# DeltaNet in chunks of 64 with hash-routed experts: a new order for the first phase, unread products in idle time, Gram blocks laid out by ScalarE, a narrower join and another opening

## The chip, the cores and the metric

The kernel runs on one core of a Trainium2 chip. The metric is the device time of one execution in microseconds (us), from runs of the same kernel. TensorE (PE) multiplies, VectorE (DVE) and ScalarE (ACT) work element by element, GpSimd (POOL) fills, copies and issues its own DMAs, SyncE (SP) issues most DMAs. Each engine carries out its instructions in the order in which they were emitted, and waits at one whose inputs are not there.

## The reference

Attention first: 4 batches and 8 heads make 32 independent recurrences over 768 tokens with a 48x48 state each. Then every token goes through the one expert that a hash of its id picks.

```python
k_n = k / (norm(k) + 1e-6)
for t in range(768):
    y[t] = q[t] @ state
    state = state + beta[t] * outer(k_n[t], v[t] - k_n[t] @ state)
x = y.transpose(0, 2, 1, 3).reshape(3072, 384)       # 8 heads x 48 side by side
e = (token_id * 2654435761) % 8
out = relu(x @ w1[e]) @ w2[e]                        # w1: 8x384x1024, w2: 8x1024x384
```

## The kernel before

**Two phases.** The first computes the attention and scatters the rows of `x`, sorted by expert, to `x_scratch` in DRAM. The second takes the experts one after the other: two dense matrix products each (lines L993 and L1023), with the result scattered to the output (L1030). It begins when the last row of `x` has been written and read back.

**The first phase by chunks.** The 768 tokens are cut into 12 chunks of 64 (`NU`), and two chunks make a group (`GC`), so there are 6 groups. On the partitions stand 64 tokens of each of two batches; the other two batches (`g2`) and the heads stand in the free dimension. For every chunk:

- `load` brings K, Q and V by DMA (L343), `turn` transposes K and Q on PE (L359) and ACT copies them to SBUF (`KQ`, L366).
- `gram` makes K K^T and K Q^T (PE, L386). The 64x64 Gram matrix of a chunk is kept as four 32x32 blocks. ACT copies the upper right block to `N12` (L398) and the left column, times a mask, to `GK` (L402); then DVE adds the lower right block into `GK` (L406), so that `GK` holds the two diagonal blocks. DVE masks K Q^T to `MT` (L411).
- `inverse`, once a group: DVE transposes `GK` to `NT` (L438), makes norms and factors (L440 to L465, with one root on ACT, L444), and inverts the 32x32 triangular blocks in 31 steps of two instructions each (L475 product into `tmp`, L473 sum into `U`). Each step needs the one before. `U` was filled with zeros by ACT (L435). `turn_back` transposes `U` on DVE to `TN` (L488) and `TU` (L490).
- `join` puts two 32x32 inverses together to one of 64x64, `TT`: PE L505, ACT to `Z` (L524), PE L514, ACT to the right half of `TT` (L530). The left half is a masked ACT copy of `TU` (L519). `Z` has an identity in its right half, so that the second product writes the upper right block and the lower right block in one go (64 rows).
- `chunk` is the recurrence: `ask` reads the state with K (PE L543), DVE subtracts from V (`R`, L558; V was scaled in L424), PE multiplies by `TT` (L566), ACT copies `W` (L577), PE updates the state (L588), ACT copies it to `S` in four pieces (L602). The answers `psY` (L543 with Q, L566 with `MT`) go by ACT to `x_sb` (L612), POOL adds the row's number (L617) and scatters it (L618).

Buffers tie the groups together: there are two `U`, one `TU` and one `TN`, four `N12`, five `KQ` and five `MT`. So group g+2 can't be inverted before group g has been turned back and joined.

**The order.** No engine's order is written by hand. Every piece of work is a `task` with an engine, a cost in ns, what it reads and writes; `order()` plays the tasks through with these costs and gives the sequence in which they are emitted. A task's priority is the length of the chain of work behind it (`rest`). There is no clock in it: a product costs the same at all times. A task of `routing` (L645, one DVE chain that sorts the tokens) takes part like the others. Matrix products that need a PSUM bank take one of those that are free at that moment.

**The opening.** POOL makes the identity and fills `S` and `x_sb` with zeros (L805, L807). ACT issues eight small DMAs for the token ids (L895), then one for `beta` (L900). DVE converts index tables (L910, L911).

Of the kernel before, what the change touches and what calls it, by code (L numbers as in the profile page):

```python
# [13 lines left out]
ACT = mybir.ActivationFunctionType  # L14
ALU = mybir.AluOpType
# [5 lines left out]
def kernel(  # L21
# [79 lines left out]
    with ExitStack() as phase1:  # L101
# [10 lines left out]
        SEED, SPREAD, PATIENCE = 1, 0.0, 0.2  # L112
        N_K, N_Q, N_V, N_KQ, N_MT, N_N = 5, 2, 3, 5, 5, 4
# [31 lines left out]
        Zs = tiles(1, "Z", [P, NS, CK])  # L145
# [41 lines left out]
        def task(eng, ns, reads, writes, emit, words=0, kb=0, more=0, boost=0, job=None,  # L187
                 hold=0, claim=(), room=()):
            deps = {writer[r] for r in reads if r in writer}
            for w in (*writes, *room):  # L190
                deps |= readers.get(w, set())
                if w in writer:
# [5 lines left out]
                              claim=claim))  # L198
# [18 lines left out]
        def order():  # L217
# [17 lines left out]
            rest = [x + t["boost"] + chance.uniform(-SPREAD, SPREAD)  # L235
# [12 lines left out]
            done = []  # L248
# [20 lines left out]

            while len(done) < n:  # L270
                best, can = None, {}
# [9 lines left out]
                pick = max((i for x, i in r if x <= at), key=lambda i: rest[i])  # L281

                soon = [x for x, i in r
                        if at < x < at + PATIENCE * tasks[pick]["ns"] and rest[i] > rest[pick]]
                if soon:
                    fits = [i for x, i in r if x <= at and tasks[i]["ns"] <= min(soon) - at + 60]
                    if fits:
                        pick = max(fits, key=lambda i: rest[i])
                    else:
                        free[e] = min(soon)  # L290
                        continue
                t = tasks[pick]
                ready[e] = [p for p in ready[e] if p[1] != pick]
                s = at
                if t["words"]:
# [7 lines left out]
                    issued += t["words"]  # L303
                start[pick] = s
                for b in t["claim"]:
                    banks[b] = None
                free[e] = s + t["ns"]
                end[pick] = s + t["ns"]
# [24 lines left out]
            return sorted(done, key=lambda i: (start[i], i)), start  # L333
# [16 lines left out]
        def turn(what, c, g2):  # L350
# [6 lines left out]
            def go():  # L357
                for u in range(HU):
# [4 lines left out]
            task("PE", 560, held(what, n, c, (g2,)), (f"j{job}",), go, words=8, job=job,  # L363
                 room=(f"KQ{c % N_KQ}.{a}.{g2}",))
            task("ACT", 490, (f"j{job}",), (f"KQ{c % N_KQ}.{a}.{g2}",),
                 lambda: nc.scalar.activation(KQ[:, HU * g2:HU * g2 + HU, a], view(), ACT.Copy),  # L366
                 job=job)

        def gram(c, g2, parts=(0, 1)):
# [4 lines left out]
            job = new_job(2 if parts == (0,) else 1 if parts == (1,) else 3,  # L374
                          early=c < 6, pair=True)
# [6 lines left out]
            def go():  # L382
                for u in range(HU):
# [7 lines left out]
            task("PE", 1000 if len(parts) == 2 else 600, need, (f"j{job}",), go, words=64, job=job,  # L391
                 room=((f"N{c % N_N}.{g2}", f"GK{g % 2}.{cc}.{g2}") if 0 in parts else ())
                 + ((f"MT{c % N_MT}.{g2}",) if 1 in parts else ()))
            gk = GK[:, :, x0:x0 + H]
            n12 = N12[:, H * g2:H * g2 + H]
            if 0 in parts:
                task("ACT", 320, (f"j{job}",), (f"N{c % N_N}.{g2}",),
# [733 lines left out]
```

## Time and profile before

| | us |
|---|---|
| runs | 600.21, 607.21, 607.65 (median 607.21) |
| profiled execution | 604.45 |
| its span, first to last instruction | 602.9 |
| PE, DVE, ACT, POOL busy | 496.7, 276.2, 140.2, 136.9 |

The span is cut below into stretches that begin and end where a group of inverses is done. Busy times of DVE are unions: neighbours overlap by about 0.1 us, so the distance between two starts is shorter than the duration. [...]

### The profile page before, as it was taken

The page shows a single profiled execution, that of the slowest core. Times are in us where ns is not written, and L with a number is a line of the kernel's source. Part 1 is how long each engine was busy: PE and PEld are TensorE (multiplying, and loading weights), DVE is VectorE, ACT ScalarE, POOL GpSimd, SP SyncE. Part 2 cuts the span into 40 slices and gives each one's busy share as a digit, 9 for nine tenths or more (in the row PEclk, how much of TensorE's full clock was granted, in tenths as well). Part 3 has the DMA queues.
Part 4 walks back from the last instruction along what each step waited for, and adds up shares of the span by engine and source line. Part 5 has one row for each costly group of instructions (what it writes and reads, how often), then busy time and mean ns, then how long its engine had stood idle before and what let it go on. Part 6 is the DMA issues. An engine that isn't in the chain of part 4 may idle for free. (4 is left out here: it accounts for less than half of the span.)

```text
span 602.9 us, 14839 instructions
## 1 busy us (share of the span) xinstructions
PE 496.7 (82%) x6340; PEld 385.1 (64%) x6340; DVE 276.2 (46%) x740; ACT 140.2 (23%) x271; POOL 136.9 (23%) x160
## 2 busy tenths in 40 slices
PE   4960399988299798549895799999999999999992
PEld 3850398877289788448794466565757676767650
DVE  6689976888984486994200122211212121212100
ACT  4451145554134563213331000101000000000000
POOL 3002301110000110100112001707161525252531
PEclk9995558898756986855888699999999999999996
DMA  5674022453113231010612985426170808000001
GB/s 105 124 138 113 2 42 67 91 115 65 45 29 77 63 82 42 28 22 22 205 64 73 289 235 145 151 51 232 33 256 12 274 13 276 12 24 14 26 23 27
DMA packets 106019, 55.85 MB, mean 93 GB/s; under 512 B 93364, under 2 KB 102013, under 8 KB 105056
## 3 DMA queue, kind: packets, MB, share of 16 engines
q1 hardware_dynamic: 100240, 45.12, 30.1%
q0 software_dynamic: 5472, 9.65, 4.5%
q8 instruction: 50, 0.82, 0.6%
q10 hardware_dynamic: 240, 0.12, 0.1%
q14 instruction: 17, 0.14, 0.1%
HBM read 44.51 MB, written 10.62 MB: 91 GB/s over the span
## 5 line engine op out<-in xcount | busy, mean ns | idle before, releaser
L993 PE MATMUL h_ps<-xT,w_sb 128*128 128x424 f32 (+3 forms) x384 | 130.3, 500 | 11.0 <-DMA xr<-x_scratch 11.0
L1030 POOL DMA_INDIRECT out_dram<-o_sb,idx x90 | 87.6, 973 | 162.7 <-DVE o_sb L1025 90.2
L993 PEld LDWEIGHTS h_ps<-xT,w_sb 128*128 128x128 f32 x384 | 74.3, 194 | 65.0 <-issue 27.8
L1023 PE MATMUL o_ps<-h_sb,w_sb 128*128 128x424 f32 (+3 forms) x336 | 112.3, 494 | 0.0
L1023 PEld LDWEIGHTS o_ps<-h_sb,w_sb 128*128 128x128 f32 x336 | 84.4, 251 | 27.2 <-issue 0.3
L618 POOL DMA_INDIRECT x_scratch<-x_sb,slot x24 | 24.1, 1006 | 232.0 <-ACT x_sb L612 188.5
L996 ACT ACTIVATE h_sb<-h_ps 128x424 f32<-128x424 f32 (+3 forms) x32 | 15.9, 497 | 233.5 <-PE h_ps L993 233.5
L998 DVE TENSOR_SCALAR h_sb<-h_ps 128x424 f32<-128x424 f32 (+3 forms) x32 | 18.1, 564 | 109.3 <-PE h_ps L993 109.3
L475 DVE TENSOR_TENSOR tmp<-U,Ni 128x112 f32<-128x112 f32 (+15 forms) x186 | 60.6, 336 | 2.5
L473 DVE TENSOR_TENSOR U<-U,tmp 128x112 f32<-128x112 f32 (+15 forms) x186 | 60.6, 337 | 2.4
L1025 DVE STREAM_TRANSPOSE o_sb<-o_ps 128x384 f32<-128x384 f32 (+2 forms) x21 | 15.5, 738 | 84.3 <-PE o_ps L1023 84.3
L505 PE MATMUL psZ<-TN,N 32*32 32x32 f32 x448 | 12.0, 218 | 33.5 <-DVE TN L488 32.8
L558 DVE TENSOR_TENSOR R<-V,psX 128x384 f32<-128x384 f32 x22 | 12.0, 547 | 51.7 <-PE psX L543 32.7
L505 PEld LDWEIGHTS psZ<-TN,N 32*32 32x32 f32 x448 | 10.7, 132 | 34.9 <-DVE TN L488 21.7
L566 PE MATMUL psX<-R,TT 64*64 64x48 f32 x704 | 29.9, 248 | 3.5 <-DVE R L558 1.9
L566 PE MATMUL psY<-W,MT 64*64 64x48 f32 x768 | 31.9, 240 | 0.0
L566 PEld LDWEIGHTS psX<-R,TT 64*64 64x64 f32 x704 | 28.0, 164 | 5.5 <-ACT root L444 2.1
L566 PEld LDWEIGHTS psY<-W,MT 64*64 64x64 f32 x768 | 29.2, 156 | 2.2 <-issue 1.2
L386 PE MATMUL psZ<-KQ 48*64 48x128 f32 (+1 forms) x576 | 24.9, 321 | 6.0 <-ACT N L398 4.0
L543 PE MATMUL psX<-S,KQ 128*64 128x96 f32 x352 | 25.9, 305 | 2.4 <-ACT S L602 2.4
L617 POOL COPY x_sb<-number 128x4 f32<-128x4 f32 x24 | 14.2, 590 | 49.4 <-DVE U L473 49.3
L386 PEld LDWEIGHTS psZ<-KQ 48*64 48x64 f32 x576 | 19.8, 166 | 8.3 <-ACT N L398 5.2
(155 smaller groups left out, 582.1 us busy)
## 6 DMA issues: line engine op xcount, KB each, us to landing
w_sb<-in_moe_w_dram SPq DMA_DIRECT2D x14, 1536.0 KB, 12.1
K<-in_k_dram SPq DMA_DIRECT2D x48, 96.0 KB, 3.1
Q<-in_q_dram SPq DMA_DIRECT2D x48, 96.0 KB, 3.2
V<-in_v_dram SPq DMA_DIRECT2D x48, 96.0 KB, 2.7
xr<-x_scratch SPq DMA_DIRECT2D x16, 145.5 KB, 3.3
w_sb<-in_moe_w_dram SPq DMA_DIRECT2D x3, 512.0 KB
w_sb<-in_moe_w_dram SPq DMA_DIRECT2D x4, 384.0 KB, 9.4
out_dram<-o_sb,idx POOLq DMA_INDIRECT x90, 2.2
```

Source lines behind the costliest of these rows:

```text
L386: nc.tensor.matmul(view()[rows(p), r, u, a0:a1], lhsT=KQ[half(r), HU * g2 + u, 0, rows(p)], rhs=KQ[half(r), HU * g2 + u, a0:a1, rows(p)], ...
L473: nc.vector.tensor_tensor(U[:, n:, 0:n], U[:, n:, 0:n], t, op=ALU.add)
L475: nc.vector.tensor_tensor(t, U[:, j:n, 0:n].to_broadcast([P, m, n]), Ni[:, j, n:, None].to_broadcast([P, m, n]), op=ALU.mult)
L505: nc.tensor.matmul(bank(one)[part(p, 1), C * x:C * x + C], lhsT=N12[part(p, 0), x], rhs=TN[part(p, 0), x0 + x], start=(x == 0), stop=True, ...
L543: nc.tensor.matmul(out[rows(p), 2 * D * u:2 * D * u + 2 * D], lhsT=KQ[:, HU * g2 + u, a, rows(p)], rhs=S0[:, p, HU * g2 + u], start=(u == ...
L566: nc.tensor.matmul(out[rows(p), D * h:D * h + D], lhsT=left[rows(p), H * g2 + h], rhs=right[rows(p), g2, D * h:D * h + D], start=(fresh an ...
L618: put = nc.gpsimd.indirect_dma_start(out=x_dram[:, :], out_offset=bass.IndirectOffsetOnAxis(ap=slot[:, col:col + 1], axis=0), in_=x_sb.rea ...
L993: nc.tensor.matmul(h_ps[:, :width], lhsT=w1_sb[:, co, fo * P:(fo + 1) * P], rhs=xT[:, co, :width], start=(co == 0), stop=(co == CO - 1))
L996: nc.scalar.activation(h_sb[:, fo, :width], h_ps[:, :width], ACT.Relu)
L998: nc.vector.tensor_scalar(out=h_sb[:, fo, :width], in0=h_ps[:, :width], scalar1=0.0, scalar2=None, op0=ALU.max)
L1023: nc.tensor.matmul(os_ps[i][:, 0:width], lhsT=w2_sb[:, fo, i::CO], rhs=h_sb[:, fo, 0:width], start=(fo == 0), stop=(fo == FO - 1))
L1030: scat = nc.gpsimd.indirect_dma_start(out=out_q, out_offset=bass.IndirectOffsetOnAxis(ap=idx[e][:, k:k + 1], axis=0), in_=o_sb[:, k], in_o ...
```

## The change

- **Costs and clock in the planner.** Task costs are set anew (for example products of 64 rows 980 ns for 1050). `order()` keeps a sum of the recent work of PE (`act` of each task), and takes 1.85 times the cost where this sum is below `warm` (after 30 us of plan time). Changing the kind of product costs 150 ns; staying with a kind gets a bonus in priority.
- **Priorities.** Each task has a tag and each tag an addition to its priority (`boosts`, from -204000 to 596500 ns). On DVE the head of an inverse and its steps stand highest, `MT` loses its place above all others, V is low. On ACT `S` and `W` stand above `GK` and `x`.
- **DVE's patience.** DVE waits for a more urgent task up to 45 ns; before, up to a fifth of the task at hand.
- **Unread products.** Where the plan leaves PE idle for over 260 ns (or has it slow) and the sum is short, after 40 us of plan time, a 128x128x128 product of the identity with itself is put into a free bank. Nobody reads it.
- **Gram blocks by ACT.** The masked ACT copy and the DVE addition (L402, L406) become three ACT copies: the left column for all partitions, then the lower right block over it for partitions 32 to 63 and 96 to 127.
- **Narrower join.** `Z` loses its identity half, the second product writes 32 rows. The lower right block comes into `TT` by a second masked ACT copy of `TU`; the upper right one by two ACT copies of 32 partitions.
- **Opening.** `beta` comes first on ACT's queue; the eight DMAs of the token ids go to POOL's queue, behind the index tables. POOL fills `U`; ACT fills `S` and `x_sb`, from 24 us of plan time on. The identity in `Z` is not made.

```diff
+        boosts = {"GK": 378500, "KQ": -25500, "MT": 67000, "N12": -30000, "R": 51500,
+                  "S": 596500, "TT": -146500, "TT12": 292000, "V": -28000, "W": 443000,
+                  "Z": -204000, ..., "head": 496000, "late": 2500, "own": 28500,
+                  "route": 134000, "solve": 500, "step": 344500, ..., "x": 374500}
...
-            rest = [x + t["boost"] + chance.uniform(-SPREAD, SPREAD)
+            rest = [x + t["boost"] + boosts.get(t["tag"], 0) + chance.uniform(-SPREAD, SPREAD)
...
+            def rate(x):
+                return 1.0 if activity(x) >= model["warm"] or x < 30000 else 1.85
...
+                span = model["wait"] if e == "DVE" else PATIENCE * tasks[pick]["ns"]
...
+                if e == "PE":
+                    gap = at - free[e]
+                    short = model["warm"] * 1.15 - activity(at)
+                    b = choices(dict(pair=False, early=False))
+                    if (at > model["fill"] and b and b[0] <= free[e] and short > 0
+                            and (gap > 260 or rate(at) > 1) and (gap > 260 or t["act"] < 0.45 * t["ns"])):
+                        ns = 215 * rate(free[e])
+                        ...
+                            tasks.append(dict(eng="PE", ns=ns, tag="fill", kind="full", at_bank=at_bank,
+                                              emit=lambda at_bank=at_bank: unread(at_bank)))
...
+        def unread(at_bank):
+            nc.tensor.matmul(homes[at_bank][:, 0:P], lhsT=ident, rhs=ident, start=True,
+                             stop=True, skip_group_check=True)
...
+                for i, (at, col) in enumerate(((slice(0, P), 0), (part(0, 1), C),
+                                               (part(1, 1), C))):
+                    task("ACT", 400, ..., lambda at=at, col=col: nc.scalar.activation(
+                             gk[at], view()[at, :, :, 0, col:col + C], ACT.Copy),
+                         job=job, tag="GK")
-                task("ACT", 400, ..., lambda: nc.scalar.activation(
-                         gk.rearrange("p j (u r) -> p r u j", r=2), view()[:, :, :, 0, 0:C],
-                         ACT.Copy, scale=kmask[:, 0:1]), job=job)
-                task("DVE", 340, ..., lambda: nc.vector.scalar_tensor_tensor(
-                         out=gk.rearrange("p j x -> p x j"), in0=n12, scalar=kmask[:, 1:2],
-                         in1=gk.rearrange("p j x -> p x j"), op0=ALU.mult, op1=ALU.add))
-                task("DVE", 600, ..., boost=1e6, job=job)            # MT
+                task("DVE", 610, ..., job=job, tag="MT")
...
-            task("ACT", 900, (), (f"U{i}",), lambda: nc.scalar.activation(
-                U, zero[:, :, None].to_broadcast([P, C, C]), ACT.Copy))
+            task("POOL", 1000, (), (f"U{i}",), lambda: nc.gpsimd.memset(U, 0.0))
...
-                            bank(two)[rows(p), C * x:C * x + C], lhsT=Z[part(p, 1), x],
+                            bank(two)[part(p, 0), C * x:C * x + C], lhsT=Z[part(p, 1), x],
...
+            for s_ in range(2):
+                task("ACT", 610, ("TU",), (f"TT{c % 3}.{s_}",), lambda s_=s_: nc.scalar.activation(
+                    TT[:, :, C * s_:C * s_ + C], TU[:, x0:x0 + NS], ACT.Copy,
+                    scale=kmask[:, s_:s_ + 1]), tag="TT")
+            for p in range(2):
+                task("ACT", 500, (f"j{two}", f"TT{c % 3}.1"), (f"TT{c % 3}.{2 + p}",),
+                     lambda p=p: nc.scalar.activation(TT[part(p, 0), :, C:], ...), tag="TT12")
...
-            dv("tensor_copy", rows_i, frm, more=9000, **on)
+            dv("tensor_copy", rows_i, frm, more=3000, **on)
...
+            nc.scalar.dma_start(out=beta_h, in_=beta.rearrange("b h s -> (b h) s"))
             make_identity(nc, ident)
...
-                        nc.scalar.dma_start(
+                        nc.gpsimd.dma_start(
                             out=tid32[w:w + NTC].rearrange("(c g) i w -> g c i w", g=2)[g2],
```

## Rows read from the trace of the kernel before

**Rows 1.** The page's span in 40 equal slices of 15.1 us: busy tenths of DVE and the granted clock of PE in tenths.
```profile
DVE  6689976888984486994200122211212121212100
...
PEclk9995558898756986855888699999999999999996
```

**Rows 2.** Busy time of each engine by stretch (us from the span's start), cut where inverses are done; then granted clock, DMA share and GB/s. In brackets the number of instructions.
```profile
30.00:75.00 45.00, 16.12 (x293) 13.28 (x295) 41.95 (x141) 12.08 (x24) 8.95 (x1) 0.66 0.42 85
75.00:110.00 35.00, 33.06 (x774) 30.20 (x768) 24.63 (x74) 17.12 (x33) 2.55 (x4) 0.66 0.29 59
110.00:163.00 53.00, 39.26 (x958) 34.61 (x954) 47.32 (x149) 22.13 (x45) 7.48 (x12) 0.88 0.38 82
163.00:208.00 45.00, 39.84 (x986) 37.39 (x988) 25.90 (x51) 20.26 (x38) 3.54 (x6) 0.69 0.26 56
208.00:261.00 53.00, 36.25 (x856) 32.61 (x850) 44.86 (x138) 18.37 (x37) 6.54 (x10) 0.79 0.18 44
261.00:291.00 30.00, 24.71 (x528) 23.77 (x528) 20.69 (x43) 7.52 (x14) 1.18 (x2) 0.52 0.10 22
291.00:326.00 35.00, 30.48 (x900) 28.68 (x896) 2.71 (x7) 13.07 (x26) 7.57 (x13) 0.90 0.38 129
...
341.00:594.00 253.00, 249.94 (x761) 164.59 (x759) 46.66 (x82) 16.33 (x33) 92.63 (x93) 1.00 0.37 114
```

**Rows 3.** The same view of the three stretches that begin when PE takes up the first group of a pair and end when the granted clock rises.
```profile
68.30:95.50 27.20, 24.67 (x510) 23.23 (x512) 18.82 (x55) 9.62 (x18) 0.00 (x0) 0.50 0.17 31
...
165.20:191.00 25.80, 24.08 (x498) 22.75 (x500) 15.38 (x40) 8.71 (x16) 1.18 (x2) 0.50 0.20 41
...
263.40:290.00 26.60, 23.68 (x498) 22.77 (x499) 17.57 (x40) 7.03 (x13) 1.18 (x2) 0.50 0.11 25
```

**Rows 4.** PE's instructions in order of time around the rise of the clock at 191 us: start, duration of the pile, line, tiles, shape and count.
```profile
182.70 1.92 PE L566 MATMUL psY<-W,MT 64*64 64x48 f32 x32
184.55 1.92 PE L514 MATMUL psZ<-TU,Z 32*64 32x32 f32 x32
186.40 2.83 PE L543 MATMUL psX<-S,KQ 128*64 128x96 f32 x32
...
193.47 0.69 PE L505 MATMUL psz<-TN,N 32*32 32x32 f32 x32
194.09 1.14 PE L566 MATMUL psX<-R,TT 64*64 64x48 f32 x32
```

**Rows 5.** The second product of the join at the full clock, in order of time.
```profile
104.67 1.12 PE L514 MATMUL psz<-TU,Z 32*64 32x32 f32 x32
```

**Rows 6.** Who waited for whom, over the whole span: DVE's waits of the first phase; us in total, times, longest.
```profile
DVE R L558 <- PE psX L543: 32.7, 6, 10.2
DVE MT L411 <- ACT GK L402: 16.0, 12, 4.2
DVE R L558 <- ACT TT L530: 12.2, 1, 12.2
DVE GK L406 <- ACT N L398: 5.7, 11, 1.4
```

**Rows 7.** DVE's busy time in line L406 alone, by the stretches of rows 2 (then clock, DMA share, GB/s).
```profile
30.00:75.00 45.00, 2.83 (x4) 0.66 0.42 85
...
110.00:163.00 53.00, 3.00 (x5) 0.88 0.38 82
...
208.00:261.00 53.00, 2.86 (x4) 0.79 0.18 44
```

**Rows 8.** The opening in order of time. SPq and ACTq are DMA issues by these engines, with the time that the issues took.
```profile
0.94 8.00 SPq L343 DMA_DIRECT2D K<-in_k_dram  x8
...
1.16 6.75 ACTq L895 DMA_DIRECT2D tid<-in_moe_token_ids_dram  x8
...
5.00 1.09 PE L359 MATMUL psz<-ident,K 128*128 128x128 f32 x4 [5.00 <-DMA K<-in_k_dram]
...
10.42 0.58 ACT L366 ACTIVATE KQ<-psz 128x512 f32<-128x512 f32 x1
...
12.31 0.13 DVE L645 TENSOR_SCALAR rt<-tid 128x32 int32<-128x32 int32 x1
...
14.23 1.11 PE L359 MATMUL psY<-ident,K 128*128 128x128 f32 x4
...
21.29 1.24 DVE L438 STREAM_TRANSPOSE NT<-GK 128x1024 f32<-128x1024 f32 x1
...
24.89 0.69 DVE L411 TENSOR_TENSOR MT<-psX,mask 128x512 f32<-128x512 f32 x1 [1.32 <-PE psX L386]
...
29.99 0.18 DVE L475 TENSOR_TENSOR tmp<-U,Ni 128x31 f32<-128x31 f32 x1
```

**Rows 9.** Two ACT copies of one Gram block, back to back, in order of time.
```profile
12.26 0.71 ACT L402 ACTIVATE GK<-psX,kmask 128x256 f32<-128x256 f32 x1 [0.77 <-PE psX L386]
...
12.77 0.41 ACT L398 ACTIVATE N<-psX 128x256 f32<-128x256 f32 x1
```

**Rows 10.** The DMAs that POOL issues for the rows of `x` (128 rows each): ns of an issue min/median/max, first and last start; then us from issue to landing.
```profile
L618 POOL DMA_INDIRECT x_scratch<-x_sb,slot x24: 977/981/1214, 96.0 to 325.5; - x24
...
DMA to landing us min/median/max: 2.6/2.9/6.9
```

**Rows 11.** The last transpose of an inverse, in order of time.
```profile
288.82 1.94 DVE L490 STREAM_TRANSPOSE TU<-U 128x1024 f32<-128x1024 f32 x1
```

More of the change, by code (lines that the diff above doesn't have):

```diff
@@ L112 @@
         SEED, SPREAD, PATIENCE = 1, 0.0, 0.2
+        WINDOW, CHANGE = 3413.0, 150.0
+        model = dict(warm=1300.0, keep=6126.5, fill=40000.0, wait=45.0)
+        boosts = {"GK": 378500, "KQ": -25500, "MT": 67000, "N12": -30000, "R": 51500,
+                  "S": 596500, "TT": -146500, "TT12": 292000, "V": -28000, "W": 443000,
+                  "Z": -204000, "askK": 179000, "askQ": 71500, "gram0": 6000, "gram1": 135500,
+                  "head": 496000, "late": 2500, "own": 28500, "route": 134000, "solve": 500,
+                  "step": 344500, "turnK": 6500, "turnQ": 500, "update": 26500, "x": 374500}
+        V_ACT = ()
         N_K, N_Q, N_V, N_KQ, N_MT, N_N = 5, 2, 3, 5, 5, 4
@@ L247, in order @@
             banks = [0.0] * len(homes)
-            done = []
+            done, fills = [], []
+            kind, recent = None, []
             def choices(job):
@@ L498, in join @@
             x0 = NS * (c % GC)
[L499 removed]
+            one, two = new_job(1, early=c < 2), new_job(2, early=c < 2)
             def first(g2):
@@ L521, in join @@
             for g2 in range(2):
-                task("PE", 560, ("TN", f"N{c % N_N}.{g2}"), (f"j{one}",),
-                     lambda g2=g2: first(g2), words=64, job=one, room=("Z",))
+                task("PE", 530, ("TN", f"N{c % N_N}.{g2}"), (f"j{one}",),
+                     lambda g2=g2: first(g2), words=64, job=one, room=("Z",), kind="32", act=64,
+                     tag="join")
             task("ACT", 500, (f"j{one}",), ("Z",), lambda: nc.scalar.activation(
-                Z[:, :, 0:C], bank(one).rearrange("p (x y) -> p x y", y=C), ACT.Copy,
@@ L526, in join @@
-                scale=-1.0), job=one)
+                Z, bank(one).rearrange("p (x y) -> p x y", y=C), ACT.Copy,
+                scale=-1.0), job=one, tag="Z")
             for g2 in range(2):
-                task("PE", 1000, ("TU", "Z"), (f"j{two}",), lambda g2=g2: second(g2),
-                     words=64, job=two, room=(f"TT{c % 3}r",))
-            task("ACT", 500, (f"j{two}",), (f"TT{c % 3}r",), lambda: nc.scalar.activation(
-                TT[:, :, C:CK], bank(two).rearrange("p (x y) -> p x y", y=C), ACT.Copy),
-                job=two)
+                task("PE", 530, ("TU", "Z"), (f"j{two}",), lambda g2=g2: second(g2),
+                     words=64, job=two, kind="32", act=64, tag="join")
@@ L534, in s_names @@
+            for p in range(2):
+                task("ACT", 500, (f"j{two}", f"TT{c % 3}.1"), (f"TT{c % 3}.{2 + p}",),
+                     lambda p=p: nc.scalar.activation(
+                         TT[part(p, 0), :, C:], bank(two)[part(p, 0)].rearrange(
+                             "p (x y) -> p x y", y=C), ACT.Copy), job=two, tag="TT12")
         def s_names(c):
@@ L602, in chunk @@
                              lambda p=p, r=r: nc.scalar.activation(
-                                 S1[half(r), p, :, D * r:D * r + D], new[half(r), p], ACT.Copy))
+                                 S1[half(r), p, :, D * r:D * r + D], new[half(r), p], ACT.Copy), tag="S")
             for g2 in range(2):
@@ L645, in dv @@
                      lambda: getattr(nc.vector, name)(
-                         *[a() if callable(a) else a for a in args], **kw), more=more, job=job)
+                         *[a() if callable(a) else a for a in args], **kw), more=more, job=job,
+                     tag=stage[0])
             def new(shape, dtype=F32):
```

162 lines of the change are left out of this document (105 added, 57 removed).

## The prediction

> **What bounds the kernel now.** I read the slices first, then the busy times by stretch, then DVE's waits, then single piles of products. From 341 us on PE is busy 249.94 of 253 us at the full clock [rows 2]: the experts run at PE's pace, and the change touches nothing there. Everything that can be won lies ahead of it. There two limits take turns. The slices show DVE near full, then half idle, three times over [rows 1]. In 30 to 75, 110 to 163 and 208 to 261 us DVE is busy 41.95 of 45, 47.32 of 53 and 44.86 of 53 us, while PE stands idle for 60 us in all [rows 2]: two inverses run interleaved, neither is done until late, and PE has nothing to join. When the first is turned back, PE starts a burst that it fills almost wholly (24.67 of 27.20, 24.08 of 25.80, 23.68 of 26.60 us), and all three run at the low clock, 0.50 [rows 3]. Now DVE waits: 75 to 110, 163 to 208 and 261 to 291 us leave it idle for 10.4, 19.1 and 9.3 us, 38.8 in all [rows 2], with `R` behind products (32.7 us) and `MT` behind ACT's Gram copies (16.0 us) [rows 6]. After the last `TU` at 288.82 us [rows 11] only the tail of the recurrence is left until 326 us.
>
> The sum is made against the profiled execution's own 604.45 us, 1.55 over its span; it lies between the runs of 600.21 and 607.65, so nothing is added for the median of 607.21. Before's own runs spread by over 1%, so under 2% counts as no change.
>
> **The change part by part.**
>
> *Opening.* ACT makes its first K copy at 10.42 us although the transposes ended at 6.09: it was issuing eight token DMAs for 6.75 us. Freed of them it can start 4.3 us earlier. But the K loads are issued until 8.94 us and the last K transposes began at 14.23 [rows 8]; a load issued at 8.94 and landing after 2.9 us, the median of POOL's [rows 10], is there at 11.8, so between 2.4 and 4.3 us are to be had. I take 3. From `NT` (21.29) to the first step (29.99) pass 8.7 us, with DVE waiting in between for `MT` (1.32 us in the row shown) [rows 8]. With the head of an inverse first and `MT` behind it I take 2.5 more, about two such waits. What speaks against: the token DMAs move to POOL, whose issue takes 0.98 us for 128 rows and lands after 2.9 us [rows 10]. Eight from 1.8 us on land at 12.5, when they are first read now (12.31) [rows 8]: no cost. But each has 384 pieces; at three times the price they land near 28 us, and DVE, in order, would stand at the token ids with the head of the inverse queued behind. That end is +5. Sum: −5.5, between −7 and +5. `U` is now POOL's, which is busy under 9 us in each stretch [rows 2]; `S` and `x_sb` are ACT's, at a time when it is idle most of the time. Nothing for either.
>
> *The second Gram step leaves DVE.* In the full stretches 13 of them took 2.83 + 3.00 + 2.86 = 8.7 us [rows 7]. Neighbours overlap by 0.1 us, so 7.4; with a little of the 5.7 us that they waited for `N` [rows 6] I take −8. The others lie where DVE has slack: nothing. Bounds −4 and −14.
>
> *The clock.* The three bursts hold 72.4 us of PE work at 0.50 [rows 3]. A pile of 32 of L566 takes 1.92 us there and 1.14 at the full clock [rows 4], of L514 1.92 [rows 4] and 1.12 [rows 5]: 0.59 of the time. If all of it ran at the full clock, and nothing else set the pace, 72.4 x 0.41 = 30 us would go. But part of each burst is a chain through ACT and DVE that does not shrink, and the filling products must first lift the clock. They are full-size (128 x 128), as the experts' products are, which run at 1.00 throughout [rows 2]; and the rise at 191 us came right after `ask` products of 128 rows (L543), not after those of 64 or 32 [rows 4]. So I take 60%: −18. Bounds 0 and −30.
>
> [...] The rows show PE 93% busy for 25.80 us at 0.50 [rows 3]. [...]
>
> *Narrower join.* The second product writes 32 rows like the first: a pile of 32 for 0.69 us [rows 4] instead of 1.12 [rows 5], 24 piles, 0.43 x 24 = 10 us at the full clock. The piles stand largely in stretches that PE fills, but the join also waits for ACT's `Z`. I take half: −5, bounds 0 and −10.
>
> *Order.* Of DVE's 38.8 us of idle time in the three slack stretches the clock gives back about half (it is counted above). The new priorities put heads and steps first, so that one inverse is done before its sibling and PE's work is spread. I take half of the remaining 20: −10. Bounds +10 (the plan's costs are off, and engines wait in order) and −25.
>
> *What ACT takes on.* Two more Gram copies, 24 times, at 0.51 us from start to start [rows 9]: 24.5 us; a second `TT` copy and a split one, 12 times at about half a us each: 12; some 2 less for the zeros. ACT is busy 110.6 of 296 us between 30 and 326 [rows 2], so most of it is covered. On the path: three copies against two and DVE's 0.71 before `NT` come out even; one more copy before the first chunk of a group, 6 x 0.5; and now and then a `W` or `S` behind a Gram copy. +4. Without that cover, in every chunk, it would be 12 x 1.5 = +18.
>
> *Unread products.* PE is idle 76 us between 30 and 326 [rows 2], and they are meant to stand there. +1; bounds 0 and the price of the second rival.
>
> Sum: −5.5 − 8 − 18 − 5 − 10 + 4 + 1 = −41.5, so 604.45 − 41.5 = **563 us**, the first phase ending near 284 us for 326. Sizes around it run from 546 to 582.
>
> **The rivals.**
>
> *DVE becomes the only limit.* From 30 to 291 us it is busy 205 of 261 us [rows 2]. If the plan closes 70% of the 56 idle us (−39), with L406 gone in all stretches after the opening (−12), the opening (−5.5) and 8 us off the tail by clock and narrower join, the end is 540. For it: all its inputs are PE's and ACT's, which have room. Against: the two buffers of `U` and one `TU` tie the groups together. Chance 0.17; 525 to 546.
>
> *The clock stays low.* If the unread products don't lift it, the −18 falls away, and a plan made for the fast clock loses its order's gain too: −41.5 + 18 + 8 = −15, 589. For it: 25 us of dense work at 0.50. Chance 0.15; 580 to 595.
>
> *The plan does not hold.* Engines work in order, so a plan whose costs are off makes each engine wait for what the plan thought ready. The gains in DVE's time and the clock are then eaten by waits like `R`'s 32.7 us [rows 6]: 604, within 2%. Chance 0.09.
>
> *The unread products stand in the way: slower.* They are placed where the plan sees PE idle. If PE runs behind its plan, they stand in front of ready work, and each takes a bank that ACT or DVE must have read first, so PE's queue waits for those. To fill half of the 76 idle us takes 38 us of them; with no idle time left for them, the whole is added, and at the low clock more: the gain of −41.5 shrinks to −23 without the clock, and +38 makes 619. It turns into a loss from the point where some 25 us of them stand before ready work. Against: nearly 60 of the 76 us lie in the three stretches that DVE fills [rows 2], where PE has nothing to do. Chance 0.07.
>
> **How the numbers follow.** Forecast 563 with 0.52, the rivals 0.17, 0.15, 0.09 and 0.07. The forecast's lower half, most of the DVE case and most of the low-clock case are to be inside: 532 to 596. Faster by over 2% (under 595) are the forecast, the DVE case and nearly all of the low-clock case: 0.83. Within 2%: 0.10. Slower: 0.07.
>
> **What would show it.** Right: no L406; PE's granted clock 1.00 through most of 60 to 280 us, with single 128-column products of the identity in the gaps; a pile of 32 of L566 near 1.14 us after the first `TN`; the second `TN` of a pair well after the first; the first step before 26 us. Wrong: token ids read after 20 us with DVE idle in front; bursts at 0.50 as in [rows 3]; `MT` or `R` with waits as in [rows 6]; unread products that wait for ACT. The whole prediction fails if the gain of the clock and that of the order are the same time counted twice, or if the second phase moves.

## The result and the profile after

The changed kernel takes 580.87 us (median of 4 runs, 579.72 to 581.99) against 607.43 us of the kernel before beside it: a ratio of 0.959, 95% interval 0.951 to 0.966. It is faster, by 26.6 us. Medians here and below are over all runs; the ratios leave out two slow runs, one of b2 (590.85 us) and one of e4 (585.55 us), each about 2% above the fastest of its kernel. The profiled execution took 580.16 us, span 578.6, which is 24.3 us under the 604.45 us against which the sum was made; the sum had 41.5. It splits without remainder worth naming: the first step of the first inverse starts at 27.5 instead of 30.0 us (−2.5), from there to the end of the last `TU` it takes 245.7 instead of 260.8 us (−15.1), and from there to the last copy into `x_sb` 27.3 instead of 33.9 us (−6.6).

The page's slices, of 14.5 us each here, busy tenths of DVE and the granted clock:
```profile
DVE  4579966787868886868011211122112121212100
...
PEclk9977558799879896889595999999999999999996
```
Of the three full stretches of DVE with holes between them [rows 1] the second and the third are gone: after two slices at 9 it is at 6 to 8 tenths from 72 us to the end of the phase. The first block of the low clock is still there (58 to 87 us); in place of the other two stand shorter dips. In the records of both traces the granted clock stands at 1.00 or at 0.50. The first record is at 22.9 us here and at 30.6 us in the kernel before; up to there the row shows 1.00, but four transposes of L419 take 1.06 to 1.12 us until 22.8 us, as at 0.50 (1.11 at 38.88 us), and 0.60 to 0.66 from 23.41 to 32.15 us.

The same view as [rows 2], cut where the inverses are done (us; PE, PEld, DVE, ACT and POOL busy; granted clock, DMA share, GB/s):
```profile
30.00:70.00 40.00, 17.18 (x199) 15.88 (x200) 36.80 (x124) 15.84 (x30) 0.78 (x1) 0.67 0.40 81
70.00:100.00 30.00, 26.93 (x613) 24.22 (x612) 19.55 (x68) 14.85 (x28) 3.66 (x7) 0.65 0.23 49
100.00:145.00 45.00, 36.55 (x1094) 33.49 (x1094) 35.74 (x101) 31.98 (x63) 5.36 (x9) 0.92 0.41 85
145.00:191.00 46.00, 39.94 (x1041) 36.68 (x1040) 36.36 (x105) 30.50 (x61) 7.22 (x11) 0.89 0.40 86
191.00:236.00 45.00, 38.22 (x932) 34.14 (x929) 33.97 (x98) 24.25 (x47) 6.21 (x9) 0.81 0.18 42
236.00:273.00 37.00, 30.94 (x873) 27.91 (x870) 30.88 (x73) 14.21 (x27) 6.03 (x10) 0.85 0.13 40
273.00:301.00 28.00, 25.41 (x610) 23.46 (x610) 1.62 (x6) 11.38 (x21) 3.54 (x6) 0.71 0.39 137
317.00:570.00 253.00, 249.46 (x760) 164.31 (x758) 46.77 (x82) 16.32 (x33) 92.22 (x93) 1.00 0.36 114
```
The experts are untouched (PE busy for 249.46 of 253 us, 249.94 before). From 100 to 236 us PE and DVE are now both busy for 34 to 40 of every 45 us, stage after stage, instead of one waiting for the other in turn. ACT has 24 to 32 us of work in such a stage.

The `TN` transposes, one for each inverse done, in order of time (the last four of six):
```profile
145.75 1.98 DVE L563 STREAM_TRANSPOSE TN<-U 128x1024 f32<-128x1024 f32 x1
...
190.81 1.93 DVE L563 STREAM_TRANSPOSE TN<-U 128x1024 f32<-128x1024 f32 x1
...
236.09 1.94 DVE L563 STREAM_TRANSPOSE TN<-U 128x1024 f32<-128x1024 f32 x1
...
268.50 1.95 DVE L563 STREAM_TRANSPOSE TN<-U 128x1024 f32<-128x1024 f32 x1
```
They stand 45.1, 45.3 and 32.4 us apart. The second pair of the kernel before:
```profile
163.09 1.90 DVE L488 STREAM_TRANSPOSE TN<-U 128x1024 f32<-128x1024 f32 x1
...
191.10 2.01 DVE L488 STREAM_TRANSPOSE TN<-U 128x1024 f32<-128x1024 f32 x1
```
There the two of a pair came 25 to 30 us apart (28.0 here) and then none for 65 or 70 us. From the third group on PE now gets one group to join at a time, 32 to 52 us behind the last. The first two are still a pair, 29.1 us apart (65.07 and 94.17).

DVE's waits over the first 301 us (us in total, times, longest), to be set beside [rows 6]:
```profile
DVE R L638 <- ACT TT L610: 19.7, 1, 19.7
DVE MT L472 <- ACT GK L463: 15.5, 10, 4.1
DVE R L638 <- PE psX L623: 10.4, 7, 4.4
DVE MT L472 <- PE psS L445: 7.7, 2, 6.4
...
DVE NT L513 <- ACT GK L463: 4.0, 5, 1.0
...
DVE MT L472 <- PE psZ L445: 3.4, 5, 1.6
```
`R` behind PE's `ask` fell from 32.7 to 10.4 us. Part of the 32.7 is no matter of the phase's order, for 12.2 us of it stand behind the last `TU` (10.21 in this row, 1.95 at 305.47):
```profile
316.23 0.56 DVE L558 TENSOR_TENSOR R<-V,psX 128x384 f32<-128x384 f32 x1 [10.21 <-PE psX L543]
```
Up to the last `TU` it fell from 20.6 to 10.4 us, and that is what the new order shows here. The 19.7 us stand in the tail, where DVE has nothing else to do. But `MT` behind ACT's Gram copies stayed at 15.5 us (16.0), and `NT`, the head of an inverse, now waits for those copies too.

### The profile page after: what moved, and what is told of

Same layout as the page of the kernel before. It is cut to its first block, busy times and chain, and to the rows that moved or that the text cites. A ratio compares the mean times of both kernels' runs of the same rounds, so it can differ in the third digit from the quotient of the medians.

```text
span 578.6 us, 15132 instructions
## 1 busy us (share of the span) xinstructions
PE 492.4 (85%) x6466; PEld 381.0 (66%) x6466; DVE 259.2 (45%) x715; ACT 179.2 (31%) x342; POOL 134.3 (23%) x169
## 5 line engine op out<-in xcount | busy, mean ns | idle before, releaser
L1078 PE MATMUL h_ps<-xT,w_sb 128*128 128x424 f32 (+3 forms) x384 | 130.0, 499 | 11.1 <-DVE xT L1060 11.1
L701 POOL DMA_INDIRECT x_scratch<-x_sb,slot x24 | 24.3, 1014 | 191.9 <-ACT x_sb L695 156.5
L548 DVE TENSOR_TENSOR U<-U,tmp 128x252 f32<-128x252 f32 (+15 forms) x186 | 61.9, 340 | 3.2
L550 DVE TENSOR_TENSOR tmp<-U,Ni 128x252 f32<-128x252 f32 (+15 forms) x186 | 61.5, 337 | 3.1
L463 ACT ACTIVATE GK<-psZ 32x256 f32<-32x256 f32 (+1 forms) x48 | 29.1, 606 | 18.5 <-DVE MT L472 10.1
L646 PE MATMUL psY<-W,MT 64*64 64x48 f32 x768 | 29.4, 230 | 0.0
L580 PE MATMUL psZ<-TN,N 32*32 32x32 f32 x384 | 9.3, 207 | 23.1 <-DVE TN L563 18.3
L646 PEld LDWEIGHTS psY<-W,MT 64*64 64x64 f32 x768 | 26.9, 146 | 1.9 <-issue 0.7
L445 PE MATMUL psZ<-KQ 48*64 48x128 f32 (+1 forms) x544 | 21.5, 305 | 6.4 <-ACT KQ L426 3.9
L638 DVE TENSOR_TENSOR R<-V,psX 128x384 f32<-128x384 f32 x22 | 11.8, 546 | 30.1 <-ACT TT L610 19.7
L580 PEld LDWEIGHTS psZ<-TN,N 32*32 32x32 f32 x384 | 8.2, 122 | 24.9 <-DVE TN L563 18.7
L623 PE MATMUL psX<-S,KQ 128*64 128x96 f32 x352 | 21.0, 270 | 3.6 <-ACT S L684 3.6
L595 ACT ACTIVATE TT<-TU,kmask 128x512 f32<-128x512 f32 x24 | 16.1, 716 | 22.2 <-DVE TU L565 22.1
```

Source lines behind the costliest of these rows:

```text
L445: nc.tensor.matmul(view()[rows(p), r, u, a0:a1], lhsT=KQ[half(r), HU * g2 + u, 0, rows(p)], rhs=KQ[half(r), HU * g2 + u, a0:a1, rows(p)], ...
L463: lambda at=at, col=col: nc.scalar.activation(gk[at], view()[at, :, :, 0, col:col + C], ACT.Copy),
L548: nc.vector.tensor_tensor(U[:, n:, 0:n], U[:, n:, 0:n], t, op=ALU.add)
L550: nc.vector.tensor_tensor(t, U[:, j:n, 0:n].to_broadcast([P, m, n]), Ni[:, j, n:, None].to_broadcast([P, m, n]), op=ALU.mult)
L580: nc.tensor.matmul(bank(one)[part(p, 1), C * x:C * x + C], lhsT=N12[part(p, 0), x], rhs=TN[part(p, 0), x0 + x], start=(x == 0), stop=True, ...
L623: nc.tensor.matmul(out[rows(p), 2 * D * u:2 * D * u + 2 * D], lhsT=KQ[:, HU * g2 + u, a, rows(p)], rhs=S0[:, p, HU * g2 + u], start=(u == ...
```

## The experiments

The interval of a ratio against the kernel before is the yardstick throughout, because that kernel's own median differs between chips (602.74, 607.69 and 604.45 us in the three groups of runs). The first four runs keep the planned order of the changed kernel to the last instruction and undo one part each.

**e1: no unread products.**
```
 def unread(at_bank):
-    nc.tensor.matmul(homes[at_bank][:, 0:P], lhsT=ident, rhs=ident, ...)
+    return None
```


> The changed kernel with its order kept, but none of the 63 unread products is emitted. They took 27.8 us of PE's busy time in the changed kernel. Theory 1 (what was won is work taken off DVE's chain; the unread products pay for the clock what the clock gives): 576 to 586 us against 580.9, with more low clock and less PE work. Rival 2 (the raised clock is what won): bursts fall to the low level again, 590 to 600 us. Rival 3 (the unread products stand in front of ready work): 565 to 575 us.

Measured: 574.79 us, ratio 0.9556 (0.9522 to 0.9590). The changed kernel itself has 0.9588 (0.9511 to 0.9664) and, once more below, 0.9546 (0.9478 to 0.9614). So the unread products are worth nothing that can be measured; the intervals leave room for some 5 us either way. The ratio is in the range of theory 1; the time is 1 us under that range and in theory 3's, but the kernel before is faster on this chip as well (602.74 us). What they do in the changed kernel is seen around the first join, PE's instructions in order of time:
```profile
45.37 4.62 PE L392 MATMUL psZ<-ident 128*128 128x128 f32 x34
67.03 1.07 PE L580 MATMUL psZ<-TN,N 32*32 32x32 f32 x32 [17.04 <-DVE TN L563]
68.03 2.50 PE L392 MATMUL psZ<-ident 128*128 128x128 f32 x10
...
89.40 0.88 PE L646 MATMUL psY<-W,MT 64*64 64x48 f32 x12
```
the same two places in e1, the first join and the first `psY` product behind it:
```profile
65.46 1.92 PE L579 MATMUL psZ<-TN,N 32*32 32x32 f32 x64 [21.76 <-DVE TN L562]
...
83.67 1.84 PE L645 MATMUL psY<-W,MT 64*64 64x48 f32 x32
```
and the windows of the changed kernel from there to 91 us, first all of it, then line L392 alone (PE and PEld, clock, DMA share, GB/s):
```profile
67.00:91.00 24.00, 23.08 (x498) 21.27 (x500) 14.58 (x53) 12.97 (x24) 1.11 (x2) 0.50 0.08 16
...
67.00:91.00 24.00, 5.74 (x20) 4.56 (x20) 0.50 0.08 16
```
Thirty-four of their 126 instructions (63 products) run straight after PE's last real work, then PE idles for 17 us until `TN`, and the first burst still runs wholly at 0.50, as in [rows 3]. Inside it 20 more take 5.74 of PE's 23.08 us, the first ten of them between the two halves of a join that are ready: the planner places them not only in gaps but also where it has PE slow. From the first join to that `psY` product pass 22.4 us, in e1 18.2. They do raise the mean clock of the phase, as this view from the first step to the last `TU` shows, first the changed kernel:
```profile
27.50:273.20 245.70, 191.18 (x4754) 173.37 (x4747) 195.93 (x574) 133.81 (x257) 29.27 (x45) 0.81 0.30 66
```
and then e1:
```profile
25.80:270.40 244.60, 181.26 (x4645) 165.27 (x4636) 196.03 (x574) 133.58 (x257) 29.24 (x45) 0.75 0.31 68
```
A clock of 0.81 against 0.75, and the same length within the spread of one kernel's executions. This is a balance: the unread products take 23.28 us of PE in this stretch, and all other products 167.9 us for 181.3 in e1, some 13 us less at the higher clock. What a higher clock would be worth without their price, e1 doesn't show.

**e2: the Gram block laid by DVE again.** One masked ACT copy and two additions by DVE straight out of PSUM take the place of the three ACT copies. (The step of before added one 128x256 piece out of `N12`.)
```
-    nc.scalar.activation(gk[at], view()[at, :, :, 0, col:col + C], ACT.Copy)     # three times
+    nc.scalar.activation(gk, view()[:, :, :, 0, 0:C], ACT.Copy, scale=kmask[:, 0:1])
+    for r in range(2):
+        nc.vector.scalar_tensor_tensor(out=gk[:, r], in0=view()[:, r, :, 0, C:2 * C],
+            scalar=kmask[:, 1:2], in1=gk[:, r], op0=ALU.mult, op1=ALU.add)
```


> The changed kernel with its order kept; the lower right Gram block goes back to DVE (two additions of 128x128 from PSUM in place of two ACT copies). DVE gets some 24 x 0.6 = 14 us of work. Theory 1: 588 to 596 us. Rival 2 (DVE has room, the clock is what won): 579 to 584 us.

Measured: 574.07 us, ratio 0.9545 (0.9509 to 0.9580), the same as the changed kernel's. Against the 607.43 us of the first chip the ratio is 579.8 us: 8 us under theory 1's range and in rival 2's, though rival 2's reason, the clock, is another matter (e1). Windows from its first step to its last `TU`:
```profile
26.30:268.80 242.50, 184.18 (x4755) 165.56 (x4748) 208.02 (x614) 111.42 (x216) 31.12 (x45) 0.84 0.31 68
```
DVE has 12.1 us more work (208.02 against 195.93) and the stretch is no longer: its idle time fell from 49.8 to 34.5 us. ACT has 22.4 us less. DVE's waits in e2 show where the idle time went:
```profile
DVE MT L481 <- ACT GK L461: 14.8, 8, 4.3
...
DVE R L647 <- PE psX L632: 3.6, 4, 2.7
DVE MT L481 <- PE psS L445: 2.8, 1, 2.8
DVE MT L481 <- PE psZ L445: 1.8, 2, 1.6
```
`R` behind PE fell from 10.4 to 3.6 us, `MT` behind PE from 11.1 to 4.6, and the 4.0 us of `NT` behind the Gram copies are gone. I read this as work that was taken off DVE, given to ACT, and came back as waits for ACT and for what ACT feeds; the waits behind PE are put down to ACT by argument alone. The time itself sinks the theory that the gain is work taken off DVE's chain.

**e3: the wide join again.** `Z` has its identity half, the second product has 64 columns of weights, and one ACT copy lays its result.
```
-    bank(two)[part(p, 0), C * x:C * x + C], lhsT=Z[part(p, 1), x],
+    bank(two)[rows(p), C * x:C * x + C], lhsT=Z[part(p, 1), x],
```


> The changed kernel with its order kept; the join is wide again (identity half of Z, second product of 64 rows, one ACT copy each to TT in place of two). The second product costs 0.43 us more a pile, 10 us in all, ACT 12 us less. Theory 1, in which PE has room between inverses: 580 to 584 us. Rival 3 (PE and its clock set the pace): 587 to 592 us.

Measured: 585.43 us, ratio 0.9706 (0.9669 to 0.9743), above both measurements of the changed kernel. A pile of 32 of the second product in the tail of the changed kernel:
```profile
289.07 0.69 PE L589 MATMUL psZ<-TU,Z 32*32 32x32 f32 x32
```
and of e3:
```profile
294.31 1.12 PE L589 MATMUL psZ<-TU,Z 32*64 32x32 f32 x32
```
The narrower pile is 0.43 us shorter, as forecast. 0.9706 against 0.9588 or 0.9546 is 1.2 to 1.6% of 607, some 7 to 10 us. It is the one part whose removal alone is seen, though the interval of the first measurement of the changed kernel comes close. ACT has 12.0 us less to do in e3 (121.8 us from first step to last `TU`) and PE 17.7 us more (208.9), and that stretch is 5 to 11 us longer than in the two traces of the changed kernel. That speaks for rival 3, in which PE's time counts for the end: against 607.43 us the ratio is 589.6 us, in its range.

**e4: token ids on ACT's queue again.**
```
-    nc.gpsimd.dma_start(out=tid32[w:w + NTC]..., in_=...)
+    nc.scalar.dma_start(out=tid32[w:w + NTC]..., in_=...)
```


> The changed kernel with its order kept; the eight token DMAs are issued by ACT again, behind beta. ACT's first copy comes about 4 us later. If the opening's gain goes through to the end: 583 to 585 us; if it is absorbed by later waits: 580 to 582 us.

Measured: 580.89 us, ratio 0.9571 (0.9518 to 0.9624): nothing that can be seen; the two ranges expected lie closer together than the runs of one kernel. The first step stands at 27.5 us with them on either queue. What holds the opening now is seen in the changed kernel, in order of time:
```profile
1.75 4.33 POOL L985 DMA_DIRECT2D tid<-in_moe_token_ids_dram  x8
...
3.25 0.17 DVE L999 CAST low_f<-low_i 128x3 f32<-128x3 int32 x1
3.33 0.24 DVE L1000 CAST iota_f<-iota_i 128x128 f32<-128x128 int32 x1
...
6.17 0.60 ACT L426 ACTIVATE KQ<-psz 128x512 f32<-128x512 f32 x1 [3.96 <-PE psz L419]
...
8.60 1.86 ACT L463 ACTIVATE GK<-psX 128x256 f32<-128x256 f32 x3 [0.50 <-PE psX L445]
...
19.97 1.23 DVE L513 STREAM_TRANSPOSE NT<-GK 128x1024 f32<-128x1024 f32 x1
```
ACT's first K copy came 4.25 us earlier (6.17 for 10.42). The token ids are half of that: in e4 it stands at 8.28. The rest fits ACT's zeros for `U`, which ran for 2.00 us from 8.52 in the kernel before, ahead of the K copy, and which POOL now makes. But `NT` came only 1.3 us earlier (19.97 for 21.29) [rows 8]: ACT lays each Gram block in three copies, 1.86 us in a row, and four blocks of them stand before `NT`.

These four explain some 7 to 10 of 26.6 us. What they leave is the order. I formed a fourth theory: the larger half of the gain is the order alone. The next runs swap scheduler and tasks.

**b2: the tasks of before under the scheduler of after.** Gram step, join, clearing and token queue as before; boosts, traced clock, price of a change of kind and unread products as after.
```
-    for i, (at, col) in enumerate(((slice(0, P), 0), (part(0, 1), C), (part(1, 1), C))):
-        task("ACT", 400, ..., tag="GK")
+    task("ACT", 400, ..., scale=kmask[:, 0:1]), job=job, tag="GK")
+    task("DVE", 340, ..., nc.vector.scalar_tensor_tensor(out=..., in0=n12, ...), tag="GK")
...
-    Zs = tiles(1, "Z", [P, NS, C])
+    Zs = tiles(1, "Z", [P, NS, CK])
...
```


> The tasks of before (left Gram column by ScalarE and the rest added by VectorE, 64-row second product with the identity half of Z, U and S cleared as before, token ids on ScalarE's queue) under the scheduler of after with its boosts, clock and unread products. Theory 4 (the order carries the larger half): 584 to 592 us, ratio 0.97 to 0.98, so that it and the narrow join make up after's gain. Rival (the boosts fit only the new tasks): 596 to 612 us, ratio 0.99 to 1.015.

Measured: 584.91 us, ratio 0.962 (0.951 to 0.973), a little better than theory 4 had it; the rival is missed. The new order with its unread products gives 22.8 us, where the changed kernel has 29.9 in the same group (r0, below); the two intervals overlap. Windows from first step to last `TU`, first of the kernel before:
```profile
30.00:290.80 260.80, 189.04 (x4369) 171.69 (x4369) 205.34 (x592) 97.48 (x189) 30.23 (x35) 0.72 0.28 60
```
and of b2:
```profile
28.60:275.70 247.10, 201.57 (x4678) 183.74 (x4679) 209.09 (x592) 98.53 (x194) 31.95 (x39) 0.79 0.31 65
```
The same 592 instructions of DVE in 13.7 us less: its idle time goes from 55.5 to 38.0 us. `R` behind `ask` waits 12.3 us in b2 up to the last `TU`, where it waited 20.6.

**b1 and b3: the new tasks under the scheduler of before.** No boosts but the old one on `MT`, one clock, no price for a change, no unread products. b1 has a patience of 0.3 of a task, b3 the old 0.2 and a claim for each solve's bank. b1 lacks that claim: its second solve can write a bank in which an early Gram block still stands, so a part of its output is changed, and its time is the weaker evidence.
```
-    boosts = {"GK": 378500, "KQ": -25500, ...}
+    boosts = {}
...
-    return 1.0 if activity(x) >= model["warm"] or x < 30000 else 1.85
+    return 1.0
...
-    claim=((3, 4) if g2 == 0 else ()) if c == 0 else ())
+    claim=(3 + g2,) if c == 0 else ())      # b3 alone
```


> All the changed tasks (Gram blocks by ScalarE, narrow join, lighter opening), but ordered as the scheduler of before orders: no traced clock, no cost for a change of kind, no boosts but the old one on MT, the same patience on every engine (0.3 of a task), no unread products. Its plan interleaves two inverses again, as before's does. Theory 4 (the order, inverses one behind the other, carries the larger half of the gain): the parts alone keep what the narrow join showed (about 7 us) and little else, so 590 to 600 us, ratio 0.98 to 0.99, with two TN transposes close behind each other and a wait of near 95 us to the next pair. Rival (the parts carry it, the order is worth nothing): 576 to 584 us, ratio near 0.96. Rival (the old order is better for the new tasks): under 574.

> The changed tasks under the scheduler of before with its own patience of 0.2 (the run with 0.3 gave 616.8 us, ratio 1.018) and with each of the first chunk's two solves claiming its own PSUM bank, which that run lacked: there the second solve could write a bank in which an early Gram block still stood, so a part of its output was changed. Theory 4 (the order carries the gain, and without it the new tasks are worth nothing): 592 to 618 us, ratio 0.98 to 1.02, inverses two at a time. Rival (the run before was slow for its patience or its bank, and the parts carry the gain): 576 to 586 us, ratio 0.95 to 0.965.

Measured: b1 616.81 us, ratio 1.018 (1.011 to 1.026), slower than each of its three expectations; b3 605.87 us, ratio 1.002 (0.998 to 1.006), as theory 4 had it. Without the order the new tasks, the narrow join among them, are worth nothing. b3 beside e1 is the plainest pair: the same tasks, no unread products in either, a mean clock of 0.74 and 0.75, and, but for the claim of one bank, only the order differs. The ratios are 1.002 and 0.956. b3's windows, first from first step to last `TU`, then two stretches of it:
```profile
27.80:295.30 267.50, 170.24 (x4416) 151.73 (x4418) 193.80 (x568) 130.21 (x249) 25.90 (x41) 0.74 0.28 59
...
110.00:166.00 56.00, 32.50 (x858) 28.00 (x854) 45.48 (x137) 27.12 (x55) 6.12 (x9) 0.89 0.37 78
...
166.00:215.00 49.00, 41.73 (x1071) 38.01 (x1072) 22.96 (x45) 27.29 (x51) 5.54 (x9) 0.71 0.25 52
```
The pattern of before is back: PE idle for 23.5 of 56 us while DVE works on two inverses, then DVE idle for 26.0 of 49. DVE's work is 11.5 us less than before's, its idle time 18.2 us more (73.7). Two of its waits:
```profile
DVE R L634 <- PE psX L619: 36.0, 11, 13.9
DVE MT L468 <- ACT GK L459: 23.2, 17, 3.6
```
`MT` behind the Gram copies went from 16.0 [rows 6] to 23.2 us and `R` from 32.7 to 36.0, of which 21.1 stand ahead of the last `TU`: as much as in the kernel before.

**b4 and b5: which half of the scheduler.** b4 keeps the boosts and takes out the clock, the prices and the unread products; b5 does the reverse, with the old boost on `MT`.
```
-    model = dict(warm=1300.0, keep=6126.5, fill=40000.0, wait=45.0)      # b4
+    model = dict(warm=1300.0, keep=0.0, fill=1e12, wait=45.0)
...
-    boosts = {"GK": 378500, "KQ": -25500, ...}                           # b5
+    boosts = {}
```


> After's tasks and boosts, but the scheduler knows nothing of the clock: every product at one duration, no price for a change of kind, no weight for staying with a kind, no unread products. Theory 4a (what orders well are the boosts, which put one inverse behind the other): 572 to 582 us, ratio 0.94 to 0.96. Rival 4b (the traced clock in the plan carries it): 588 to 606 us, ratio 0.97 to 1.0.

> After's tasks, clock, prices of a change of kind and unread products in the scheduler, but no boosts other than the old one on MT. Theory 4a (the boosts carry the order): 590 to 612 us, ratio 0.975 to 1.01. Rival 4b (the traced clock carries it): 574 to 584 us, ratio 0.945 to 0.96.

Measured: b4 591.96 us, ratio 0.976 (0.967 to 0.985); b5 595.17 us, ratio 0.984 (0.975 to 0.993). b4 came out as rival 4b had it (the clock carries it), b5 as theory 4a had it (the boosts carry it). The two contradict each other: neither half carries it alone. Both intervals lie below 1, neither by a clear 2%; 2.4 and 1.6% add up to about the whole (4.1 to 4.5%). The windows of b5 from first step to last `TU` (the clock is the figure behind POOL's),
```profile
29.40:285.40 256.00, 187.71 (x4738) 168.26 (x4739) 196.24 (x573) 133.14 (x254) 26.40 (x41) 0.84 0.29 61
```
show 0.84, above the changed kernel's 0.81, and the stretch is 10.3 us longer; its order is another too, so the clock is not all that differs.

**c1: e1 and e2 together**, with after's order.

> After's order with two edits of the runs before put together: no unread products, and the Gram block laid by one masked ScalarE copy and two VectorE additions. If each is worth what it showed against after (0 to 6 us each) and they add: 566 to 573 us, ratio 0.935 to 0.95. If both gains are one and the same (ScalarE's queue freed at the same places), or are drift of the chip: as either alone, 572 to 578.

**r0: the changed kernel once more**, in the same group as c1, b1 and b2.

> The changed kernel itself once more, as the yardstick of this group, because the level of the kernel before differs from chip to chip (607.4 and 602.7 us so far). Every theory: ratio 0.95 to 0.966, about 576 to 582 us.

Measured: c1 569.58 us, ratio 0.9425 (0.9345 to 0.9505); r0 577.78 us, ratio 0.9546 (0.9478 to 0.9614). c1's median is 8.2 us below the changed kernel's on the same chip and the lowest of all runs here, but the two intervals still overlap. It lies in the range for two gains that add. Its window:
```profile
24.20:266.30 242.10, 178.66 (x4668) 161.90 (x4664) 208.08 (x614) 111.30 (x217) 28.91 (x45) 0.77 0.32 69
```
A clock of 0.77 against e2's 0.84, and the stretch is as long (242.1 and 242.5 us); e2's unread products take 21.7 us of PE in it. DVE idles for 34.0 us. The same view of r0's profiled execution:
```profile
26.90:278.30 251.40, 196.53 (x4754) 176.87 (x4747) 195.98 (x574) 133.93 (x256) 29.99 (x45) 0.79 0.30 65
```

The stretch from first step to last `TU`, gathered from the windows above, with DVE's idle time as length less busy time:

| tasks | order | length | DVE busy | DVE idle | mean clock |
|---|---|---|---|---|---|
| before | before | 260.8 | 205.3 | 55.5 | 0.72 |
| before | after (b2) | 247.1 | 209.1 | 38.0 | 0.79 |
| after | before (b3) | 267.5 | 193.8 | 73.7 | 0.74 |
| after | after | 245.7 | 195.9 | 49.8 | 0.81 |
| after, once more (r0) | after | 251.4 | 196.0 | 55.4 | 0.79 |
| after, no unread products (e1) | after | 244.6 | 196.0 | 48.6 | 0.75 |
| after, Gram by DVE (e2) | after | 242.5 | 208.0 | 34.5 | 0.84 |
| the same, no unread products (c1) | after | 242.1 | 208.1 | 34.0 | 0.77 |

Each row is one execution, and executions of one kernel differ: the one profiled of r0 took 585.68 us where the others took 577 to 579, and its stretch is 5.7 us longer than the changed kernel's first. So differences of some 6 us between rows are not shown. The order is worth 13.7 us on the old tasks and 16 to 22 on the new, which is beyond that. With either order the new tasks take 11.5 or 13.2 us of work off DVE and put 18.2 or 11.8 us of idle time in its place; the lengths gain nothing beyond the spread.

## Why the prediction was right, and which of its terms were not

The direction, the place of the gain and the range held: the second phase didn't move, the gain lies ahead of the experts, and 580.87 is inside 532 to 596. The likeliest time was 18 us too low. Two large terms of the sum were not there, and a third was undersized; that these errors stand against each other, and that the range is 64 us wide, is the luck in it.

*Order: −10 forecast, and the mechanism was right.* The prediction had one inverse done before its sibling, and from the third group on so it is. With the unread products it is worth 22.8 us (b2), within its bounds of +10 to −25 and more than twice what I took. As e1 finds the unread products worth nothing, I put all of it down to the order; on the new tasks b3 and e1 show the order without them, 4.6%. Of the 32.7 us of `R`'s waits that I set against the slack stretches, 12.2 stood in the tail. I took half of what the clock would leave over. It can't be cut that way: b4 and b5 show that neither the boosts nor the traced clock in the plan gives the whole, and I take it that the traced clock, too, works through the order.

*The clock and the unread products: −18 and +1 forecast, about 0 found for the two together.* Two steps failed: that 60% of the 72.4 us of PE work at 0.50 would go over to the high clock and shrink, and that what was to bring this about would cost +1, as products that stand in PE's idle time. The mean clock rose (0.75 in e1, 0.81 in the changed kernel; 0.77 in c1, 0.84 in e2), and the other products took some 13 us less. But the unread ones took 23.3 us of PE in the same stretch, 5.74 of them in the first burst (2.50 in front of a join that was ready), which they didn't lift and which took 4.2 us longer; and the end came no earlier. That PE's time was worth nothing doesn't follow: e3 gave PE more work and was slower. The prediction named as its way to fail that clock and order are the same time counted twice. On the new tasks e1 has the order at nearly the old clock (0.75 for 0.72) and the whole gain, so there the order needs no raised clock; on the old tasks no run took the order with the clock held low.

In the first burst of the changed kernel neither dense work nor 128-row products lifted the clock: PE is busy for 23.08 of 24.00 us at 0.50 from 67 to 91 us, 5.74 of them with 128-row products.

*The second Gram step off DVE: −8 forecast, and +4 for ACT's copies.* The arithmetic of DVE's work was right: e2 puts back 12.1 us, the prediction's figure for all stretches after the opening. That this work was the limit was wrong. With the step back on DVE nothing is lost (0.9545). The two terms belong together and sum to about 0, or to a small loss, if c1's 8 us are any guide.

*Narrower join: −5, measured −7 to −10 (e3) under the new order.* Right in kind, near its bound of −10. Under the old order the whole of the new tasks gives nothing (b3), so this is no property of the join alone.

*Opening: −5.5, measured −2.5 at the first step, inside −7 to +5* (−2.3 to −4.1 in the four traces that share this opening: the changed kernel, r0, e1 and e3). ACT did start 4.25 us earlier, though only half of it for the reason given. The three Gram copies ate most of it; I had called them even. Token ids came early and not late (read at 8.52 instead of 12.31 us), so the +5 end never arose, and e4 shows that the queue doesn't matter for the end.

All terms of the planner together were −10 − 18 + 1 = −27, and b2 has 22.8 us; all terms of the tasks were −5.5 − 8 − 5 + 4 = −14.5, and from b2 to r0 it is 7.1 us.

Of the signs of being right, no L406 came. The second `TN` of a pair came well after the first, but this was no sign: it stood 25 to 30 us behind in the kernel before as well. These didn't come: a clock of 1.00 through most of the phase, the first burst at the full clock, the first step before 26 us. Of the signs of being wrong three came: the first burst at 0.50, `MT`'s waits as in [rows 6] (15.5 us), and unread products that wait for ACT, by 2.3 us (1.6 for `TT`, 0.7 for `Z`). Of the rivals "the clock stays low" (580 to 595) has the measured time just inside, as has the forecast's own band (546 to 582), and half of its reason holds: the gain of the clock fell away, but the order's didn't. "DVE only limit" (540) fails by DVE's idle time, 49.8 us and not 17.

## What to carry over

DVE was not relieved by giving its work to ACT, which feeds it: with the new tasks 11.5 or 13.2 us of work left it, and 18.2 or 11.8 us of idle time came in its place. Where an engine has gaps in its time, ask whose output ends each of its waits, and count the work there at full price. Sum the gains of order and of speed only once, and let the order be tried with the old tasks before anything is moved. Products whose only use is to raise the clock have a price like any other: here they took 23 us of PE's time, and what they sped up didn't show at the end.

## What the runs showed of the hardware

ACT and DVE take turns here at one pair of PSUM banks although both only read. In the changed kernel, in order of time:
```profile
73.50 0.61 ACT L463 ACTIVATE GK<-psS 128x256 f32<-128x256 f32 x1 [1.34 <-PE psS L445]
74.15 0.69 DVE L472 TENSOR_TENSOR MT<-psS,mask 128x512 f32<-128x512 f32 x1 [1.83 <-ACT GK L463]
...
74.88 0.60 ACT L463 ACTIVATE GK<-psS 32x256 f32<-32x256 f32 x1 [0.76 <-DVE MT L472]
```
The three don't overlap: between the end of one and the start of the next lie 0.04 us, and the trace gives each as what released the next; neither plan has that dependency. Over the first 301 us `MT` waits 15.5 us for the copies and they 12.5 us for `MT`. No run took that order away, so what two reads at the same time would do is not shown.

DVE's two casts of the opening (128x3 and 128x128, int32 to fp32) ended when POOL's run of fills ended, in the two traces where they met. In the kernel before they started at 3.26 and 3.33, took 3.57 and 3.56 us and ended by 6.89, and POOL filled `S` and `x_sb` from 2.99 to 6.80. In e4 they took 1.59 and 1.58 us and ended by 4.91, and POOL filled `U` from 2.99 to 4.82. In the changed kernel POOL was issuing the token DMAs at that time, and they took 0.17 and 0.24 us. What ties the two engines together here no run separates.
